# Scores of two heads side by side in TensorE's row halves, in an attention and mixture-of-experts kernel

## The chip, the cores and the metric

The kernel runs on one core of a Trainium2 chip (trn2). The time is the device time of one launch in microseconds: median of three runs 371.16 us (371.13 to 371.59). A profile is one more execution, recorded by the hardware profiler. Engines in its views: PE is TensorE's matmuls, PEld its weight loads (which overlap the matmuls), DVE is VectorE, ACT is ScalarE, POOL is GpSimd, SP is the sync engine that issues DMAs.

## The reference

Attention over 4 batches of 8 heads, 768 positions, 64 values a head; then a mixture of 4 experts, in which every token goes through every expert:

```python
scores = q @ k.T / sqrt(64)                    # batch 4, heads 8, seq 768, dim 64
keep   = causal                                # heads 0, 2, 6 ("retrieval")
keep   = causal & (first 4 keys | last 64)     # heads 1, 3, 4, 5, 7 ("streaming")
a      = softmax(where(keep, scores, -1e9))
x      = (a @ v).transpose(0, 2, 1, 3).reshape(3072, 512)
p      = domain_probs / sum(domain_probs)
out    = sum over e of p[:, e] * (relu(x @ w1[e]) @ w2[e])     # w1 512x1024, w2 1024x512
```

## The kernel before

**Work and its order.** A batch is cut into two chunks of 384 queries, so there are eight attention chunks. The expert network takes tiles of 128 tokens: the first three and the fourth one by one ("plain" steps, L1255), the other twenty in pairs (`pair_steps`, L1405). A pair has first layers (plain matmuls of 256 columns at L1413, or seven products in place of eight at L1442) and then one second layer, seven products of 16 matmuls with 256 columns each (L1596), whose intermediate sums ScalarE copies (L1616), and VectorE adds (L1619) and combines (L1175).

Each engine's instructions are written out by hand in one order; nothing is rescheduled afterwards. The main loop at the end walks through the expert network's steps, advances a planned clock (`tick`, L1154) and puts a step of the next attention chunk between them as long as a plan of due times (`plan`, L1779, and `att_ns`, L1768) says that the chunk is behind. Attention is therefore spread between the matmuls of the expert network. A generator that yields `WAIT` puts its step off. `require` (L1805) finishes a chunk at once where its result is needed.

**Scores.** `scores(h)` (L892) computes one head's scores of a chunk, with keys as the stationary operand and queries moving, into a bank of PSUM (`bank()`, L101: four banks, shared with the first layers), then lets ScalarE take the exponential into a tile `es` (L917), and VectorE multiply the mask in (L924, L928). Queries of two heads lie together in 128 rows (`qT`, 64 rows each). The keys of one head stand in a tile of 128 rows of which the other head's 64 rows are zeros (`kR` for the retrieval heads, `kW` for the windowed ones), so a matmul runs over all 128 rows and the zeros drop the other head's queries. A retrieval head has four score matmuls in the first chunk of a batch and eight in the second; a streaming head of batches 1 to 3 has seven windows of 56 (the first 48) queries.

**Where the keys come from.** In batches 1 to 3, POOL's DMAs load keys and queries of a chunk by rows and narrow them to 16 bits (`load_by_rows`, L218, three DMAs each), SP's DMAs transpose them (`transpose_rows`, L261: three for the keys into `kT`, three for the queries into `qT`), and VectorE copies the halves into their places (`keys_to_rows`, L273; `keys_to_windows`, L281). `kT` holds one chunk and the tail of the one before. `load_k` and `load_q` of the next chunk are issued when a chunk begins; the transposes of the next chunk after its fourth head.

**Values.** `values_r` (L937, retrieval heads) and `values` (L1010) multiply the weights by the values in PSUM tiles `pV`, and divide. Retrieval heads' results go through `x_one` or `x_pair` and a transposing DMA of SP's (L1004) into `xT`, the input of the expert network; the streaming heads' quotient is taken with a logarithm and an exponential on ScalarE (L1039, L1042), and VectorE's product (L1045) comes 1.3 us of planned clock later. `values` of a streaming head waits on the planned clock, so that two don't follow at once (`apart`). In batches 1 to 3 the heads go in the order 0, 2, 6, 1, 3, 5, 7, 4 (L1071), each head's values some heads behind its scores.

Batch 0 is different: its first chunk has an order of its own (`FRONT`, L619), its second transposes on TensorE (L798), with outputs in half of the array's columns.

Of the kernel before, what the change touches and what calls it, by code (L numbers as in the profile page):

```python
# [19 lines left out]
def kernel(  # L20
# [99 lines left out]
    for i in range(2):  # L120
        kR.append(pers.tile([P, NCH, NR, 3, P], FP16, name=f"kR{i}"))
        vR.append(pers.tile([P, S // P, NR, D + 2], FP16, name=f"vR{i}"))
# [38 lines left out]

    kT = pers.tile([P, HP, P + CH], FP16, name="kT")
    v_sinks = pers.tile([NS, 1, NSH * P], FP16, name="v_sinks")
# [16 lines left out]
    def key_tile(b, c, h, t):  # L180

        i = b % 2
        if RETR[h]:
            return kR[i][:, t // 3, RH.index(h), t % 3, :]
        if b:
            return kW[:, t, SH.index(h), :]
        return kS[:, t // TC, t % TC, SH.index(h), :]
# [29 lines left out]

    def load_by_rows(x, x16, b, c):  # L218
        for j in range(3):
            s0 = c * CH + j * P  # L220
            gp.dma_start(
                out=x16[:, j, :, :],
                in_=x[b, :, s0 : s0 + P, :].rearrange("h p d -> p h d"),
            )
# [36 lines left out]
    def transpose_rows(b, c):  # L261
        alloc_qT(b, c)
        for x, xr, at in ((kT, k_rows[b, c], P), (qTs[b, c], q16[b, c], 0)):
            for j in range(3):
                nc.sync.dma_start(
                    out=x[:, :, at + j * P : at + (j + 1) * P],
                    in_=xr[:, j, :, :].rearrange("p h d -> p (h d)"),
                    transpose=True,
                )
# [3 lines left out]
    def keys_to_rows(b, c):  # L273

        for n, hps in ((slice(0, 2), slice(0, 2)), (slice(2, 3), slice(3, 4))):
            nc.vector.tensor_copy(
                out=kR[b % 2][half(0), c, n, :, :].rearrange("p n t x -> p n (t x)"),
                in_=kT[half(0), hps, P : P + CH],
            )

    def keys_to_windows(b, c, part):  # L281

        x = kW[:, 0:WT, :, :]
        for r, n0, hp0, n in [((1, 0, 0, 2), (1, 3, 2, 2), (0, 2, 2, 1))[part]]:
            r = half(r)
            src = kT[r, hp0 : hp0 + n, P - WO + NS :]
            step = src.ap[1][0]
            src = bass.AP(
                src.tensor, src.offset, [src.ap[0], [step, n], [WQ, WT], [1, P - NS]]
            )  # L290
            dst = x[r, :, n0 : n0 + n, :].rearrange("p t n x -> p n t x")
            nc.vector.tensor_copy(out=dst[:, :, :, NS:P], in_=src)
            if c == 0:
                src = kT[r, hp0 : hp0 + n, P : P + NS]
                src = src.rearrange("p n (t x) -> p n t x", t=1)
                nc.vector.tensor_copy(
                    out=dst[:, :, :, 0:NS], in_=src.to_broadcast([D, n, WT, NS])
                )
        if part == 2 and b * NCH + c + 1 < G:
            nc.vector.tensor_copy(out=kT[:, :, P - WO : P], in_=kT[:, :, CH + P - WO :])  # L300

# [478 lines left out]
    def attention(b, c):  # L780
# [111 lines left out]
        def scores(h):  # L892
            hp = h // 2
            es_of[h] = []
            for cols, parts, masks in score_tiles(h):
                ps = bank()
                ns = 0
                for n, (t, o, q0, nq) in enumerate(parts):
                    nc.tensor.matmul(  # L899
                        out=ps[:, o : o + nq],  # L900
                        lhsT=key_tile(b, c, h, t),
                        rhs=qTs[b, c][:, hp, q0 : q0 + nq],
                        start=(n == 0 or not first),
                        stop=not first,
                        skip_group_check=first,
                    )
                    ns += mm_ns(nq)
                if first:
                    for m, mo, o0, o1 in masks:
                        bias = bC if m is mC else bSf  # L910
                        nc.tensor.matmul(
                            out=ps[:, o0:o1], lhsT=ident16,
                            rhs=bias[:, mo : mo + o1 - o0],
                            start=False, stop=True, skip_group_check=True,
                        )
                es = att.tile([P, 512], FP16, name="es", bufs=8)
                nc.scalar.activation(  # L917
                    out=es[:, 0:cols], in_=ps[:, 0:cols], func=AF.Exp, scale=SC
                )
                for m, mo, o0, o1 in () if first else masks:  # L920
                    if m is mC:
                        x = es[:, o0:o1].rearrange("p (n x) -> p n x", x=P)
                        y = mC.rearrange("p (n x) -> p n x", n=1)
                        nc.vector.tensor_tensor(  # L924
                            out=x, in0=x, in1=y.to_broadcast(list(x.shape)), op=ALU.mult
                        )
                        continue
                    nc.vector.tensor_tensor(  # L928
                        out=es[:, o0:o1],
                        in0=es[:, o0:o1],  # L930
                        in1=m[:, mo : mo + o1 - o0],
                        op=ALU.mult,
                    )
                es_of[h].append((es, parts))
                yield ns

        def values_r(h):  # L937

            ct, u = PLACE[h]
            shared = by_dma and ct  # L940
# [69 lines left out]
        def values(h):  # L1010
# [3 lines left out]
            ct, u = PLACE[h]  # L1014
            while by_dma and clock[0] < apart["until"] and not apart["rush"]:
                yield WAIT
# [32 lines left out]
            later(scale, g)  # L1049
            apart["until"] = clock[0] + 1900.0  # L1050

            yield ns + (600.0 if g == 1 else 400.0)
# [17 lines left out]
        else:  # L1070
            order = (0, 2, 6, 1, 3, 5, 7, 4) if by_dma else (0, 2, 1, 3, 6, 5, 7, 4)  # L1071
            more = divmod(g + 1, NCH) if g + 1 < G else None
# [6 lines left out]
            if by_dma:  # L1079
                keys_to_rows(b, c)  # L1080
                yield 1500.0
            else:
                yield from transposes(0)

            waiting = []
            for n, h in enumerate(order):
                v_steps, done = iter(()), None
                ahead = sum(len(score_tiles(x)) for x in (*waiting, h))
                if len(waiting) > 1 or (waiting and ahead > (6 if by_dma else 8)):
                    done = waiting.pop(0)  # L1090
                    v_steps = values(done)
                yield from both(scores(h), v_steps)
                if not by_dma and n < 2:
                    yield from transposes((1, 3)[n])
                if done is not None:
                    behind_values(done)
                waiting.append(h)
                if n < 3 and by_dma:
                    keys_to_windows(b, c, n)
                if n == 1 and by_dma:  # L1100
                    sink_rows(b, c)
                if n == 3 and more and g > 1:
                    transpose_rows(*more)
                if not by_dma and n == 2:
                    yield from transposes(2)
            if more:
                if g == 1:
                    load_probs(pair0)
                    transpose_rows(*more)
            for h in waiting:  # L1110
# [37 lines left out]
    WAIT = -1.0  # L1148
    apart = {"until": 0.0, "rush": False}

    def later(op, g):
# [253 lines left out]
    def pair_steps(nt0, nxt):  # L1405

        def plain_layer1(e):
            xs = scaled(e)
            for f0 in range(0, FTP, 2):
# [19 lines left out]
                yield 2 * DMP * mm_ns(PC), 0.5  # L1429

        s1 = moe.tile([P, 4 * HN], FP32, name="s1", tag="sums", bufs=1)
        kept = [s1[:, (n % 2) * HT * P : (n % 2 + 1) * HT * P] for n in range(3)]
# [210 lines left out]
        if ahead and three(nxt):  # L1643
            inputs_for_third()
        half = KT // 2 * mm_ns(HN), PSHARE
        yield from product(x, A11, b(0, 0), True)
        keep(0, x)
# [37 lines left out]
        if last:  # L1685

            r = slice((nt0 + 1) * P, (nt0 + 2) * P)
            for c in (slice(0, HN // 2), slice(HN // 2, HN)):
# [12 lines left out]
                nc.sync.dma_start(out=out[r, c], in_=o[:, 1, c])  # L1701
            return
        yield from product(x, A22, t(2), False)
        nc.scalar.copy(out=o[:, 1, 0:HN], in_=x)
# [48 lines left out]
    zero(gp, kR[1].rearrange("p c n t x -> p (c n) t x"))  # L1753
    gp.memset(kT[:, :, P - WO : P], 0.0)

# [12 lines left out]
    def att_ns(a):  # L1768
        ns = 4000.0 if a % NCH == 0 else 6100.0
        ns += 1000.0 if a >= NCH else 0.0  # L1770
        ns += NSH * (600.0 if a == 1 else 400.0)
        return ns + (600.0 + HP * 3 * 400.0 if a < NCH else 0.0)

# [4 lines left out]
    begin = E * UNIT + 0.6 * ONE  # L1778
    for a, n in zip(range(2, G), (0.72, 1.65, 2.95, 4.15, 5.4, 6.65)):  # L1779
        plan[a] = (begin, first_pair + n * PAIR)  # L1780
        begin = plan[a][1]
# [90 lines left out]
```

## Time and profile before

| | |
|---|---|
| median of three runs | 371.16 us |
| the profiled execution's own time | 370.57 us |
| its span, first to last instruction | 368.8 us |
| granted TensorE clock, mean | 1.000 |
| PE matmuls, 60 to 180 us / 180 to 368.8 us | 120.00 of 120.00 us / 185.82 of 188.80 us |
| VectorE in the same stretches | 92.55 / 140.96 us |
| ScalarE | 81.86 / 105.02 us |
| POOL | 57.77 / 17.43 us |
| score matmuls, L899 | 396 recorded, 141 on `kR` and 255 on `kS` |
| first chunk of batch 1 begins (copies at L276) | 78.4 us |

A PE record's end is modelled, so records of neighbours overlap, and a busy share near 1 says only that matmuls were always in flight. The distance between starts tells what a matmul cost. VectorE and ScalarE have room over the whole, which says nothing of a single moment.

### The profile page before, as it was taken

What the parts mean: (1) busy time and instruction counts of PE and PEld (TensorE: products, weight loads), DVE (VectorE), ACT (ScalarE), POOL (GpSimd) and SP (SyncE); (2) the same over time, 40 slices, a digit from 0 to 9 for tenths busy, and PEclk for the clock granted to TensorE, in tenths of its full rate; (3) what the DMA queues carried; (4) which work ended last, traced back from release to release, by engine and by line L of the source; (5) the groups of instructions that cost most, each with busy time, mean ns of one, the idle gap of its engine ahead of it and who ended that gap; (6) DMA issues with size and microseconds to landing.
All of it is one profiled execution on the core that took longest, in us unless ns stands there. A gap on an engine that the chain in (4) does not pass through costs nothing.

```text
span 368.8 us, 10367 instructions
## 1 busy us (share of the span) xinstructions
PE 362.9 (98%) x4243; PEld 309.6 (84%) x4243; DVE 278.0 (75%) x586; ACT 227.0 (62%) x477; POOL 120.6 (33%) x176
## 2 busy tenths in 40 slices
PE   7999999999999999999999999999999999999996
PEld 4755566679999999999989999988999998998996
DVE  7864875898687499778567749777758868979982
ACT  6736689348768776765767955874777361450630
POOL 7985775783166049027302731220000000000000
PEclk9999999999999999999999999999999999999999
DMA  8999999999999399999907992960220300300101
GB/s 222 193 199 206 185 195 195 168 183 116 138 93 164 93 108 141 122 120 106 150 11 90 168 129 40 124 126 2 71 69 2 116 3 2 117 2 0 60 3 57
DMA packets 119092, 39.55 MB, mean 107 GB/s; under 512 B 107024, under 2 KB 111700, under 8 KB 119044
## 3 DMA queue, kind: packets, MB, share of 16 engines
q0 software_dynamic: 82848, 18.62, 60.1%
q1 hardware_dynamic: 35108, 19.48, 24.4%
q10 hardware_dynamic: 1088, 0.79, 0.7%
q8 instruction: 33, 0.54, 0.6%
q14 instruction: 15, 0.12, 0.1%
HBM read 44.89 MB, written 6.34 MB: 139 GB/s over the span
## 4 chain that ended last, share of the span: by engine, by line
PE 86%; DMA 5%; DVE 4%; POOL 3%; issue 1%; DVEq 0%
PE pO L1596 30%; PE pA L1413 21%; PE pO L1442 9%; PE pO L1294 6%; PE pA L1247 6%; PE pA L899 5%; DMA w1sb<-in_moe_w_dram 2%; PE pV L1442 2%; PE pA L1442 2%; PE pV L957 2%; PE pV L1024 2%; DVE xs L1361 1%; DMA xT<-x_pair 1%; DMA hA<-in_k_dram 1%; POOL w1sb L330 1%; DMA hA<-in_q_dram 1%
## 5 line engine op out<-in xcount | busy, mean ns | idle before, releaser
L1596 PEld LDWEIGHTS <-hA 128*128 128x128 f16 x1104 | 104.6, 98 | 11.8
L1413 PE MATMUL pA<-xs,w1sb 128*128 128x256 f16 x768 | 97.3, 272 | 0.0
L1413 PEld LDWEIGHTS <-w1sb 128*128 128x128 f16 x768 | 71.8, 98 | 7.3
L1596 PE MATMUL pO<-w2sb,hA 128*128 128x256 f16 x640 | 77.3, 272 | 0.0
L1422 ACT ACTIVATE hA<-pA 128x512 f16<-128x512 f32 x96 | 57.1, 598 | 29.1 <-PE pA L1413 26.9
L917 ACT ACTIVATE es<-pA 128x384 f16<-128x384 f32 (+2 forms) x122 | 58.5, 513 | 21.3 <-PE pA L899 19.3
L308 POOL DMA_DIRECT2D vS<-in_v_dram x30 | 29.6, 989 | 107.4 <-PE pV L1024 105.6
L1596 PE MATMUL pO<-tsb,hA 128*128 128x256 f16 x464 | 57.0, 272 | 0.0
L1361 DVE TENSOR_TENSOR xs<-xT,pB 128x1024 f16<-128x1024 f16 (+1 forms) x49 | 46.9, 978 | 2.8 <-DMA xT<-x_pair 2.8
L1175 DVE TENSOR_TENSOR hA<-hA 128x1024 f16<-128x1024 f16 x60 | 39.2, 684 | 0.5 <-PE pO L1596 0.3
L1442 PEld LDWEIGHTS <-w1sb 128*128 128x128 f16 x512 | 31.3, 98 | 1.3 <-DVE xs L1175 0.4
L1274 ACT ACTIVATE hA<-pA 128x128 f16<-128x128 f32 (+1 forms) x59 | 19.4, 377 | 19.9 <-PE pA L1247 19.6
L1294 PE MATMUL pO<-w2sb,hA 128*128 128x512 f16 x120 | 28.9, 379 | 0.0
L1247 PE MATMUL pA<-xT,w1sb 128*128 128x128 f16 (+1 forms) x236 | 27.8, 268 | 0.3 <-DMA w1sb<-in_moe_w_dram 0.3
L1616 ACT COPY s<-pO 128x256 f32<-128x256 f32 x31 | 11.6, 373 | 26.2 <-PE pO L1596 20.6
L1247 PEld LDWEIGHTS <-w1sb 128*128 128x128 f16 x256 | 19.3, 98 | 9.1 <-issue 1.2
L1045 DVE TENSOR_TENSOR xT<-pV,rc 64x384 f16<-64x384 f32 x35 | 19.4, 555 | 9.9 <-ACT rc L1042 9.2
L1039 ACT ACTIVATE rc<-pV,eps 64x384 f32<-64x384 f32 x35 | 20.1, 576 | 9.7 <-PE pV L1024 9.2
L1459 DVE CUSTOM_DVE_ANT_0 hA<-pO,s 128x512 f16<-128x512 f32 x26 | 17.7, 688 | 9.8 <-PE pO L1442 8.3
L928 DVE TENSOR_TENSOR es<-es,mS 128x384 f16<-128x384 f16 (+1 forms) x40 | 13.7, 346 | 14.9 <-ACT es L917 14.9
L1452 ACT COPY s<-pO 128x512 f32<-128x512 f32 x39 | 22.7, 588 | 2.7 <-PE pO L1442 2.3
L899 PE MATMUL pA<-qT,kR 128*128 128x128 f16 (+2 forms) x141 | 23.2, 261 | 0.0
(194 smaller groups left out, 536.9 us busy)
## 6 DMA issues: line engine op xcount, KB each, us to landing
pB<-p_rows SPq DMA_DIRECT2D x10, 512.0 KB, 7.2
out_dram<-o SPq DMA_DIRECT2D x19, 256.0 KB, 3.9
w1sb<-in_moe_w_dram POOLq DMA_DIRECT2D x16, 256.0 KB, 7.3
w2sb<-in_moe_w_dram POOLq DMA_DIRECT2D x8, 512.0 KB, 8.5
vS<-in_v_dram POOLq DMA_DIRECT2D x30, 112.0 KB, 3.9
k_rows<-in_k_dram POOLq DMA_DIRECT2D x18, 128.0 KB, 5.0
q<-in_q_dram POOLq DMA_DIRECT2D x18, 128.0 KB, 6.4
out_dram<-hA SPq DMA_DIRECT2D x4, 256.0 KB, 7.1
```

The lines of the kernel that those rows point to most:

```text
L308: gp.dma_start(out=t[:, :, own_v(h)], in_=windows_of(v, b, h, c))
L899: nc.tensor.matmul(out=ps[:, o : o + nq], lhsT=key_tile(b, c, h, t), rhs=qTs[b, c][:, hp, q0 : q0 + nq], start=(n == 0 or not first), stop ...
L917: nc.scalar.activation(out=es[:, 0:cols], in_=ps[:, 0:cols], func=AF.Exp, scale=SC)
L1175: nc.vector.tensor_tensor(out=out, in0=a, in1=b, op=ALU.subtract)
L1247: nc.tensor.matmul(out=ps[:, 0 : x.shape[2]], lhsT=w1_tile(e, CTS[n], ft), rhs=x[:, CTS[n], :], start=(n == 0), stop=(n == DMP - 1),)
L1294: nc.tensor.matmul(out=ps_o, lhsT=hs[:, ft, :].rearrange("p (x j) -> p j x", j=tiles)[:, j, :], rhs=w2sb[:, e * FTP + ft, :], start=(ft == 0),
L1361: nc.vector.tensor_tensor(out=o, in0=xin, in1=pb.to_broadcast([P, DMP, n, P]), op=ALU.mult)
L1413: nc.tensor.matmul(out=ps[:, f * PC : (f + 1) * PC], lhsT=w1_tile(e, ct, f0 + f), rhs=xs[:, ct, :], start=(ct == 0), stop=(ct == DMP - 1),)
L1422: nc.scalar.activation(out=blocks[:, b0 : b0 + 2, k0 : k0 + 2, :].rearrange("p t f x -> p f t x"), in_=ps.rearrange("p (f t x) -> p f t x" ...
L1442: nc.tensor.matmul(out=ps[:, f * P : (f + 1) * P], lhsT=w_tile(e, w[:, ct, :], f), rhs=a[:, ct, :], start=(first and f == 0 and ct == 0), ...
L1452: nc.scalar.copy(out=kept[n], in_=ps)
L1596: nc.tensor.matmul(out=ps, lhsT=a[:, k, :], rhs=b(k), start=(first and k == 0), stop=(k == KT - 1), skip_group_check=not first,)
```

## The change

In batches 1 to 3:

- Heads 0 and 2 (`TURNED`), 1 and 3, and 4 and 5 (`WINDOWED`) get their queries and keys in the two row halves of the same tile: `SLOT` puts head 2 beside head 0, and head 1 in place of it. Their score matmuls use 64 rows each, in turns of the two heads, into different banks (`scores_of_two`). Four banks are written in one go, and then their four exponentials are queued.
- A go is only begun while `wide["open"]` holds, which the second layers of a pair set and the first layers clear (it is set at the start), and when the planned clock says that ScalarE is nearly free (`by_act`).
- `kT` keeps a whole batch of keys. Heads 0 and 2 read it as it is, the windowed pairs read windows copied with both heads at once and without zero rows; heads 6 and 7 (`PADDED`) keep zero rows.
- The order within a chunk is written out anew (`in_pairs_of_heads`): goes first, then values, with heads 6 and 7 in between. The transposes of the next chunk come after the scores of all heads and the values of 0, 2, 6 and 1.
- Loading by rows takes seven DMAs in place of three, since the slots of heads 0 to 3 are out of order.
- Exponentials of heads 1, 3, 4 and 5 lie in a part of `kS` that is no longer used for keys. The plan's numbers are changed.

```diff
-    kT = pers.tile([P, HP, P + CH], FP16, name="kT")
+    kT = pers.tile([P, HP, WO + S], FP16, name="kT")
+    SLOT = (0, 2, 1, 3, 4, 5, 6, 7)
+    TURNED, WINDOWED, PADDED = (0, 2), ((1, 3), (4, 5)), (6, 7)
...
     def key_tile(b, c, h, t):
...
+        if b and h in PADDED:
+            return kR[1][:, t // 3, b % 2, t % 3, :] if RETR[h] else kW[:, t, 4, :]
+        if b:
+            r, hp = half(SLOT[h] % 2), SLOT[h] // 2
+            if RETR[h]:
+                return kT[r, hp, WO + t * P : WO + (t + 1) * P]
+            return kW[r, t, [h in x for x in WINDOWED].index(True), :]
...
     def load_by_rows(x, x16, b, c):
+        for h in range(HP):
+            gp.dma_start(out=x16[:, :, SLOT[h], :], in_=rows_of(x, b, h, c))
         for j in range(3):
             s0 = c * CH + j * P
             gp.dma_start(
-                out=x16[:, j, :, :],
-                in_=x[b, :, s0 : s0 + P, :].rearrange("h p d -> p h d"),
+                out=x16[:, j, HP:, :],
+                in_=x[b, HP:, s0 : s0 + P, :].rearrange("h p d -> p h d"),
             )
...
     def keys_to_rows(b, c):
-        for n, hps in ((slice(0, 2), slice(0, 2)), (slice(2, 3), slice(3, 4))):
+        nc.vector.tensor_copy(
+            out=kR[1][half(0), c, b % 2, :, :].rearrange("p t x -> p (t x)"),
+            in_=kT[half(0), 3, WO + c * CH : WO + (c + 1) * CH],
+        )
...
+    def keys_to_windows(b, c, n):
+        r, hp = ((slice(0, P), 1), (slice(0, P), 2), (half(1), 3))[n]
+        src = kT[r, hp, c * CH + NS :]
+        src = bass.AP(src.tensor, src.offset, [src.ap[0], [WQ, WT], [1, P - NS]])
+        dst = kW[r, 0:WT, (0, 1, 4)[n], :]
+        nc.vector.tensor_copy(out=dst[:, :, NS:P], in_=src)
...
             for cols, parts, masks in score_tiles(h):
+                while by_dma and by_act["free"] > clock[0] + 900.0 and not apart["rush"]:
+                    yield WAIT
...
+        def exponentials(h, ps, cols, parts, masks):
+            if by_dma and h in (1, 3, 4, 5):
+                n = (1, 3, 4, 5).index(h)
+                n = (2 + n // 2) * NT * P + n % 2 * CH
+                es = kSf[:, n : n + CH]
+            else:
                 es = att.tile([P, 512], FP16, name="es", bufs=8)
...
+            by_act["free"] = max(by_act["free"], clock[0]) + 650.0
+            ready[h] = by_act["free"] + 500.0
...
+        def scores_of_two(work):
+            while not (wide["open"] and by_act["free"] < clock[0] + 500.0):
+                if apart["rush"]:
+                    break
+                yield WAIT
+            done, ns = [], 220.0
+            for heads, (n, parts, masks) in work:
+                pss = [bank() for _ in heads]
+                for t, o, q0, nq in parts:
+                    for h, ps in zip(heads, pss):
+                        nc.tensor.matmul(
+                            out=ps[:, o : o + nq],
+                            lhsT=key_tile(b, c, h, t),
+                            rhs=qTs[b, c][half(SLOT[h] % 2), SLOT[h] // 2, q0 : q0 + nq],
+                            start=True,
+                            stop=True,
+                        )
+                    ns += mm_ns(nq)
+                done += [(h, ps, n, parts, masks) for h, ps in zip(heads, pss)]
+            for x in done:
+                es_of.setdefault(x[0], [])
+                exponentials(*x)
+            yield ns
+
+        def in_pairs_of_heads():
+            keys_to_rows(b, c)
+            tiles = score_tiles(TURNED[0])
+            work = [[(TURNED, x) for x in tiles[n : n + 2]] for n in range(0, len(tiles), 2)]
+            others = [(x, *score_tiles(x[0])) for x in WINDOWED]
+            yield from scores_of_two(work[0])
+            keys_to_windows(b, c, 0)
+            keys_to_windows(b, c, 1)
+            yield 200.0
+            for x in (*work[1:], others):
+                yield from scores_of_two(x)
+                yield 100.0
+            keys_to_windows(b, c, 2)
+            sink_rows(b, c)
+            yield from values(0)
+            yield from both(scores(6), values(2))
+            yield from values(6)
+            yield from both(scores(7), values(1))
+            behind_values(1)
+            if more:
+                transpose_rows(*more)
+            for h in (3, 4, 5, 7):
+                yield from values(h)
+                behind_values(h)
...
+            while not soon(h):
+                yield WAIT
...
     def att_ns(a):
-        ns = 4000.0 if a % NCH == 0 else 6100.0
...
+        if a == 1:
+            return 6700.0 + NSH * 600.0 + HP * 3 * 400.0
+        return 5300.0 if a % NCH == 0 else 7300.0
...
-    for a, n in zip(range(2, G), (0.72, 1.65, 2.95, 4.15, 5.4, 6.65)):
+    for a, n in zip(range(2, G), (0.6, 1.5, 2.55, 3.95, 5.2, 6.65)):
```

`soon(h)` is true when the planned clock has passed `ready[h]`; `values` of a streaming head asks it too, and adds 1200 to `by_act["free"]`.

## The prediction

> **What bounds the kernel now.** First the page's busy line and the chain that ended last:
>
> ```profile
> PE 362.9 (98%) x4243; PEld 309.6 (84%) x4243; DVE 278.0 (75%) x586; ACT 227.0 (62%) x477; POOL 120.6 (33%) x176
> PE 86%; DMA 5%; DVE 4%; POOL 3%; issue 1%; DVEq 0%
> ```
>
> TensorE's matmuls hold 86% of the chain, and the waiting of DMA, VectorE and POOL in it lies mostly before 30 us. So from batch 1 on, a microsecond of TensorE work removed is a microsecond of time, as long as TensorE does not wait in its place. The second view is TensorE's order of time in a stretch without gaps. Columns: start, length with a modelled end, line, operation, count. The distance from one start to the next is the true price:
>
> ```profile
> 151.84 0.34 PE L899 MATMUL pA<-qT,kS 128*128 128x48 f16 x7
> 152.03 0.61 PE L1442 MATMUL pO<-xs,w1sb 128*128 128x128 f16 x8
> 152.47 1.04 PE L1413 MATMUL pA<-xs,w1sb 128*128 128x256 f16 x8
> 153.34 0.34 PE L957 MATMUL pV<-vR,es 128*128 128x65 f16 x6
> ```
>
> Seven matmuls of a windowed head (48 and 56 columns) take 152.03 - 151.84 = 0.19 us, 27 ns each; 128 columns take 0.44/8 = 55 ns, 256 take 0.87/8 = 109 ns. Price goes by columns; that half of the contraction rows are zeros in these scores makes nothing cheaper. The third view is the same list where batch 0 uses half of the array's columns (128*64, two outputs in two halves):
>
> ```profile
> 46.59 0.82 PE L1247 MATMUL pA<-xT,w1sb 128*128 128x384 f16 x4
> 47.25 0.19 PE L957 MATMUL pV<-vR,es 128*128 128x65 f16 x1
> 47.37 0.36 PE L798 MATMUL pA<-ident,q 128*64 128x128 f16 x6
> 47.56 0.33 PE L798 MATMUL pA<-ident,k 128*64 128x128 f16 x6
> 47.83 0.61 PE L1294 MATMUL pO<-w2sb,hA 128*128 128x512 f16 x2
> ```
>
> From 47.25 to 47.83 are 0.58 us, 0.03 of them for the 65 columns. Twelve matmuls of 128 columns in turn would be 12 x 55 ns = 0.66 us, more than there is. Side by side they are 6 x 55 = 0.33 us, and 0.22 us remain for going into the half-array shape and back.
>
> **The change part by part.** *TensorE work removed.* A turned head (0 or 2) has four matmuls in a first chunk (128, 128, 256, 256 columns: 0.33 us) and eight in a second (1,920 columns: 15 x 55 = 0.82 us). Heads 0 and 2 side by side save one of the two: 3 x (0.33 + 0.82) = 3.45 us over three batches. The pairs (1,3) and (4,5) save one windowed head each, 0.185 us, in six chunks: 12 x 0.185 = 2.2 us. Together 5.65 us. The trace has no row halves; the nearest row is L798's column halves. Bounds: nothing saved, and 5.65. I take 5.65, since L798 overlapped fully.
>
> *Shape changes added.* A first chunk has two goes (one for the turned heads, one for the windowed), a second chunk three: 3 x 5 = 15 goes, each into and out of the shape, at L798's 0.22: +3.3 us. Bounds: the way in alone costs 0.12 - 0.03 = 0.09 (47.25 to 47.37), so 1.4 us if the way out is free; 5.7 us if each way costs a whole small matmul's latency (0.19).
>
> *Four banks in one go.* ScalarE must empty four banks after each go. Its back-to-back pace is:
>
> ```profile
> 111.08 1.47 ACT L917 ACTIVATE es<-pA 128x512 f16<-128x512 f32 x3 [0.49 <-PE pA L899]
> ```
>
> Three in 1.47 us with 0.60 for one alone: the next two take about 0.44 to 0.48 each. So four full banks are free about 0.27 + 0.60 + 3 x 0.48 = 2.3 us after the first of them is written, and that one is written 0.2 us before the go ends. In a second layer the next go stands at least two half products (1.74 us) and a shape change (0.1) on and uses its fourth bank last: no wait. The copies of the product (L1616) queue behind the exponentials, but the bank they empty is wanted again one whole product (1.74 us) later: hidden. In the first chunk of batch 1 the built order of the changed kernel puts the goes into the plain layers, the first 0.86 us before a first layer, which also needs these banks at 0.22 us each, the second right behind that layer's eight ReLUs. Going bank by bank, the third and fourth are about 0.1 us late each and the second go's fourth bank 0.3: +0.5 us. Bounds: 0, and 1.4 if the activations don't overlap at all (0.60, 0.60, 0.39, 0.39 and 0.28 per ReLU).
>
> *Queues of SP and POOL.* The transposes of the next chunk now stand behind the x_pair transpose of heads 2 and 6, and the next chunk's first go comes at once:
>
> ```profile
> 126.00 3.84 SPq L265 DMA_TRANSPOSE kT<-k_rows  x3
> 129.93 4.32 SPq L265 DMA_TRANSPOSE qT<-q  x3
> 134.34 1.21 SPq L1004 DMA_TRANSPOSE xT<-x_pair  x1
> ```
>
> Each takes 1.3 us of the queue, and a qT one lands 3.6 us after issue (kT: 4.8). From the end of head 6's values: 1.2 us to x_pair, 1.3 for its transpose, 6.55 until the last qT issue, 3.6 to land: 12.7 us. In the changed order the matmuls between that end and the next go are worth 14.2 us (batch 1), 12.9 (batch 1 to 2), and over 18 later. The one at 12.9 has no margin: +0.3 us, bounds 0 and 1.5 (VectorE up to a microsecond late). In exchange the x_pair transpose no longer waits behind the six. Before, it did once on the chain:
>
> ```profile
> 229.45 1.20 DVE xs L1361 x2
> ...
> 235.99 4.06 DMA xT<-x_pair
> 243.98 1.75 PE pA L1413 x16
> ```
>
> It landed at 240.05, its scaling came late, and TensorE's records have a gap of 0.31 us at 241.6: -0.3 us, bounds 0 and -0.8 (all gaps after 60 us).
>
> POOL issues 48 loads of three rows and 36 of four in place of 36 of eight, at 0.79 against 0.91 us: 67 us for 33, 5.7 us more per chunk:
>
> ```profile
> L221 POOL DMA_DIRECT2D q<-in_q_dram x18 | 16.3, 928 | 0.8 <-issue 0.8
> L306 POOL DMA_DIRECT2D vR<-in_v_dram x21 | 16.1, 786 | 4.7 <-DMA w2sb<-in_moe_w_dram 3.9 <-DMA k_rows<-in_k_dram 0.7
> L308 POOL DMA_DIRECT2D vS<-in_v_dram x30 | 29.6, 989 | 107.4 <-PE pV L1024 105.6 <-DMA k_rows<-in_k_dram 1.3 <-DMA q<-in_q_dram 0.5
> ```
>
> Its 105.6 us of waiting for values matmuls (up to 20 at a time) hide that; without this cover the queries of the second chunk of batch 1, landing at 96 to 101 where they are turned from 97 on, would cost up to 1 us. VectorE loses 7.5 us of copies (6 x 0.465 to kR, 12 x (0.646 - 0.402) to the windows, 1.2 of repeated sinks, 5 x 0.245 of carried keys); it is not on the chain there: nothing.
>
> **Sum.** -5.65 + 3.3 + 0.5 + 0.3 - 0.3 = -1.85 us. The profiled execution took 370.57 us around its span of 368.8 and lies 0.59 below the median of 371.16. Its time would be 368.7, the median's 369.3.
>
> **Rivals.** *(a) The halves overlap only partly.* In the windowed pairs a matmul lasts 27 ns and each wants its own weight load. If the loads of both halves go in turn, a pair of 56 columns lasts 54 ns and the 2.2 us vanish: 371.16 - 1.85 + 2.2 = 371.5. For it: seven loads in 0.19 us is also 27 ns a load, so the present pace may be that of loading. Against: L798's pairs keep 55 ns with two loads in them. [...]
>
> *(b) The burst is not hidden: slower.* One mechanism: ScalarE's four exponentials in a row, at every go. Masks on VectorE wait for them, and the second layers' copies (0.37), additions (0.42) and differences (0.68) stand behind in both queues. If each go makes TensorE wait 0.25 us, that is 15 x 0.25 = 3.75: 373.1. It decides from 1.85/15 = 0.12 us per go. For it: four windowed exponentials and their masks (0.35) end some 2.0 us after the go, an addition 0.42 later, and in the last batches it is wanted 2.6 us after the go: a margin of 0.2. Against: before, ScalarE is 62% busy, and its copies ran freely. [...]
>
> *(c) It doesn't do what it says:* the halves don't overlap at all. Then nothing is saved and the costs stay: 371.16 + 3.3 + 0.5 + 0.3 - 0.3 = 375.0. Against it stands L798; for it, that those halves share all 128 rows and these don't.
>
> **How the numbers follow.** Forecast 369.3: 0.54. Its own range goes from 367.4 (-5.65 + 1.4 + 0.5, the way out of the shape free and the two terms of 0.3 cancelling) to 370.4 (half of what the waits' upper bounds leave: (0.9 + 1.2)/2 = 1.05 more). (a) 371.5: 0.19. (b) 373.1: 0.20. (c) 375.0: 0.07. About 0.2%, 0.74 us, is what this kernel's measurement can tell from no change. Faster is the forecast, 0.54; of (a) 0.15 lies within 0.74 us; slower is the rest of (a), (b) and (c): 0.31. The range goes from 367.4 to 373.2, which takes in (a) and most of (b) and leaves out (c) and the tails.
>
> **What would show it.** Pairs right: two matmuls of a turned go start a few ns apart, with 55 or 109 ns to the next pair, and a windowed go has 28 matmuls in about 0.38 us. Shape changes right: 0.22 us over the matmuls' own time per go. The burst: gaps before the matmul that takes a bank, copy or sum behind an exponential, none in second layers, some 0.5 us around the two goes of batch 1's first chunk. SP: the first go of batch 2 waits for qT by less than 1.5 us, and the 0.31 us gap is gone. I am wrong if windowed pairs keep 54 ns, if a change of shape by rows costs over 0.35 us a go, or if second layers show waits of over 0.12 us per go.

## The result, and the profile after

The changed kernel took 375.72 us in the median of six executions (375.05 to 378.32), the kernel before 371.33 beside it: 1.0127 times as long, interval 1.0092 to 1.0162. It is slower by 4.4 us, where 2 us of gain were forecast.

The profiled execution took 378.32 us, its span 376.6 against 368.8 before. Its busy line and the engines' shares of the chain that ended last:

```profile
PE 365.4 (97%) x4243; PEld 306.2 (81%) x4243; DVE 274.2 (73%) x575; ACT 226.3 (60%) x477; POOL 149.6 (40%) x224
PE 61%; DMA 19%; POOL 10%; issue 6%; SPq 2%; DVE 2%; ACT 1%; POOLq 0%; ACTq 0%; DVEq 0%
```

The number of matmuls is the same (x4243), yet TensorE's share of the chain fell from 86% to 61%, and DMA's rose from 5% to 19%. The 19% are not all lost time: from 42 to 81 us the chain follows loads and transposes back while TensorE works. What TensorE loses are its waits for transfers. Who it waited for is in the view of waits (engine, line, releaser, us in total, times, longest):

```profile
PE pA L963 <- DMA qT<-q: 4.9, 2, 2.9
...
PE pO L1506 <- DVE xs L1238: 1.0, 1, 1.0
```

L963 is the matmul of a go. The two waits are the first goes of batch 1 and of batch 2. The chain in order of time (start, length, what) shows the first, then the second:

```profile
71.24 1.19 SPq L273
...
74.69 6.26 DMA qT<-q
80.95 0.14 issue
81.09 0.51 PE pA L963 x8
```

```profile
137.57 4.74 DMA qT<-q
142.31 0.04 issue
142.35 0.51 PE pA L963 x8
```

TensorE had reached these goes at 77.8 and 140.1 us. From start to start of its matmuls, the two waits are 3.07 and 2.12 us over the matmuls' own time. The third query transpose took 6.3 and 4.7 us from issue to landing, not the 3.6 of the prediction. What stood ahead of it on SP's queue the second time:

```profile
128.55 1.19 SPq L1071 DMA_TRANSPOSE xT<-x_pair  x1
129.96 3.83 SPq L273 DMA_TRANSPOSE kT<-k_rows  x3
134.01 4.79 SPq L273 DMA_TRANSPOSE qT<-q  x3
```

Before, x_pair came behind the six; now the six come behind it, and the last query transpose is issued at 137.57. A third stop is at 249 us, where the kernel before had its gap of 0.31:

```profile
246.46 2.55 DMA out_dram<-o
249.02 0.11 DVE xs L1424
...
250.55 0.62 PE pO L1506 x8
```

TensorE loses 1.20 us there. The releaser named, a store of results, is inferred from its time, and VectorE's scaling does not read it. In the code, the buffer written at L1424 is `xs1`, which takes the room of the rows of queries, `q16` (L1270). It may be written when the last three query transposes have read them, and those stood on SP's queue from 240.32 on, behind x_pair:

```profile
234.83 1.25 SPq L1071 DMA_TRANSPOSE xT<-x_pair  x1
236.30 3.81 SPq L273 DMA_TRANSPOSE kT<-k_rows  x3
240.32 5.26 SPq L273 DMA_TRANSPOSE qT<-q  x3
```

In the DMAs' completion records the last of them ends at 248.58, and the scaling begins 0.42 us later, at 249.00. `e2_three_loads` below has the same 0.42 us, from 246.10 to 246.52. So the change of SP's order comes back here as well.

A fourth loss is in the table by stretches (stretch, length, busy us of PE, PEld, DVE, ACT and POOL with counts, then granted TensorE clock, DMA share, GB/s):

```profile
77.70:81.10 3.40, 0.49 (x5) 0.04 (x3) 2.03 (x3) 0.00 (x0) 3.01 (x7) 1.00 1.70 177
81.10:85.00 3.90, 3.90 (x30) 2.67 (x31) 2.35 (x6) 2.47 (x7) 3.74 (x5) 0.57 1.09 180
85.00:140.00 55.00, 54.99 (x718) 48.34 (x716) 39.51 (x84) 42.25 (x85) 30.85 (x41) 1.00 1.21 120
140.00:142.40 2.40, 0.45 (x6) 0.24 (x6) 1.97 (x4) 1.02 (x3) 2.40 (x4) 1.00 1.52 96
142.40:147.00 4.60, 4.60 (x55) 3.20 (x55) 2.78 (x8) 2.44 (x7) 4.60 (x7) 0.63 1.24 85
```

After each of the two waits for queries TensorE ran 3.41 us at half clock (a granted clock of 0.50 from 81.68 to 85.10 and from 143.12 to 146.54; matmuls of 512 columns 427 ns apart, of 128 columns 107, against 216 and 56 at a clock of 1.00). By the table the loss is 3.9 x 0.43 + 4.6 x 0.37 = 3.4 us. Not every execution shows it: mean clocks were 0.991, 0.995, 0.999 and three times 1.000, with 378.32, 377.34, 375.06 us and 375.05 to 376.0. So the median of 375.72 lies among the executions at 1.000: the kernel is slower without the half clock too. Other runs have such waits too: the one of 2.94 us in `e12_before_go_early` was followed by a clock of 0.63 from 81.5 to 86 us, while those of 2.24 (`e1_turn_early`), 2.17 (`e2_three_loads`) and 3.13 us (`e6_windows_first`) were not followed by such a stretch in the profiled executions, whose mean clocks are 1.000, 0.999 and 0.999 (3.41 us at 0.50 would lower a mean over 375 us by 0.005). So the length of the wait alone does not tell whether half clock follows: 2.12 us had it and 3.13 us had not. What decides it was not tested.

The bill of the profiled execution: waits 3.07 + 2.12 + 1.20 = 6.4 us, half clock 3.4, together 9.8; the span grew by 7.8, so the rest gained about 2.0 us net. Most of that is the halves, which `e9_full_rows` below puts at 1.5 us. TensorE's list of a second layer (start, length with a modelled end):

```profile
110.20 0.61 PE L963 MATMUL pA<-qT,kT 64*128 64x128 f16 x10
110.75 1.05 PE L1660 MATMUL pO<-tsb,hA 128*128 128x256 f16 x8
...
115.02 0.53 PE L963 MATMUL pA<-qT,kS 64*128 64x48 f16 x28
115.49 1.05 PE L1660 MATMUL pO<-w2sb,hA 128*128 128x256 f16 x8
```

From 110.20 to 110.75 are 0.55 us for ten matmuls that would take 0.88 in turn, and 28 windowed ones take 0.47 for 0.71. By the starts, the way into the shape costs 0.096 us and the way out 0.09.

### The profile page after: what moved, and what is told of

Same layout as the page of the kernel before. It is cut to its first block, busy times and chain, and to the rows that moved or that the text cites. A ratio compares the mean times of both kernels' runs of the same rounds, so it can differ in the third digit from the quotient of the medians.

```text
span 376.6 us, 10434 instructions
## 1 busy us (share of the span) xinstructions
PE 365.4 (97%) x4243; PEld 306.2 (81%) x4243; DVE 274.2 (73%) x575; ACT 226.3 (60%) x477; POOL 149.6 (40%) x224
## 4 chain that ended last, share of the span: by engine, by line
PE 61%; DMA 19%; POOL 10%; issue 6%; SPq 2%; DVE 2%; ACT 1%; POOLq 0%; ACTq 0%; DVEq 0%
PE pO L1660 27%; PE pA L1476 16%; PE pO L1506 8%; DMA q<-in_q_dram 3%; DMA k_rows<-in_k_dram 3%; DMA qT<-q 3%; DMA w1sb<-in_moe_w_dram 2%; DMA w2sb<-in_moe_w_dram 2%; PE pV L1506 2%; SPq L273 2%; PE pA L963 2%; PE pA L1506 2%; POOL w1sb L329 1%; DMA vS<-vS 1%; POOL q L226 1%
## 5 line engine op out<-in xcount | busy, mean ns | idle before, releaser
L1660 PEld LDWEIGHTS <-hA 128*128 128x128 f16 x1104 | 105.4, 98 | 14.8 <-issue 2.1
L1476 PE MATMUL pA<-xs,w1sb 128*128 128x256 f16 x768 | 95.8, 273 | 0.0
L927 ACT ACTIVATE es<-pA 128x512 f16<-128x512 f32 (+3 forms) x98 | 45.2, 520 | 21.5 <-PE pA L900 12.5
L307 POOL DMA_DIRECT2D vS<-in_v_dram x30 | 28.2, 943 | 74.2 <-PE pV L1093 70.5
L1424 DVE TENSOR_TENSOR xs<-xT,pB 128x1024 f16<-128x1024 f16 (+1 forms) x49 | 46.8, 977 | 3.2 <-DMA out_dram<-o 3.1
L1357 PE MATMUL pO<-w2sb,hA 128*128 128x512 f16 x120 | 29.8, 387 | 0.0
L1310 PE MATMUL pA<-xT,w1sb 128*128 128x128 f16 (+1 forms) x236 | 28.9, 275 | 0.0
L1451 DVE TENSOR_TENSOR hA<-hA 128x1024 f16<-128x1024 f16 (+1 forms) x26 | 14.6, 563 | 15.0 <-ACT hA L1485 14.8
L1357 PEld LDWEIGHTS <-hA 128*128 128x128 f16 x128 | 12.5, 103 | 11.9 <-issue 0.9
```

Of the source, the lines that this page charges most:

```text
L307: gp.dma_start(out=t[:, :, own_v(h)], in_=windows_of(v, b, h, c))
L927: nc.scalar.activation(out=es[:, 0:cols], in_=ps[:, 0:cols], func=AF.Exp, scale=SC)
L1310: nc.tensor.matmul(out=ps[:, 0 : x.shape[2]], lhsT=w1_tile(e, CTS[n], ft), rhs=x[:, CTS[n], :], start=(n == 0), stop=(n == DMP - 1),)
L1357: nc.tensor.matmul(out=ps_o, lhsT=hs[:, ft, :].rearrange("p (x j) -> p j x", j=tiles)[:, j, :], rhs=w2sb[:, e * FTP + ft, :], start=(ft == 0),
L1424: nc.vector.tensor_tensor(out=o, in0=xin, in1=pb.to_broadcast([P, DMP, n, P]), op=ALU.mult)
L1476: nc.tensor.matmul(out=ps[:, f * PC : (f + 1) * PC], lhsT=w1_tile(e, ct, f0 + f), rhs=xs[:, ct, :], start=(ct == 0), stop=(ct == DMP - 1),)
```

## The experiments

All ran beside the kernel before; on their chip that took 370.8 to 370.9 us. "Early", "windows first" and "later go" are the three edits that are put together below.

**One edit of SP's order (`e1_turn_early`).**

```diff
             yield from both(scores(6), values(2))
+            if more:
+                transpose_rows(*more)
             yield from values(6)
             yield from both(scores(7), values(1))
             behind_values(1)
-            if more:
-                transpose_rows(*more)
```

> The changed kernel, with one statement moved: the six transposes of the next chunk are issued before the values of head 6, so that they stand ahead of the x_pair transpose on SP again, as in the kernel before. TensorE's order is the same to the last matmul. Theory (late queries): TensorE's wait of 2.1 us before the first go of batch 2 and the 1.2 us gap at 249 us (there VectorE writes into the room of the queries' rows, which the last three transposes must have read) both come from these transposes being late, so 3.3 us go and at most 0.3 us come back for x_pair: 372.4 to 373.0 us against the 375.7 of the changed kernel; the wait of 3.1 us before the first go of batch 1 stays, since that chunk's transposes are issued elsewhere. Rival (shape changes and bursts of exponentials cost more than costed): these are untouched, so 375.4 to 376. Rival (POOL's fourteen loads alone make the queries late): the waits stay where they are, 375.4 to 376.

372.85 us, ratio 1.0067 (1.0043 to 1.0091). The wait for queries at batch 2 and the gap at 249 are both gone from the trace, with TensorE's order unchanged: the theory held, and the third stop was SP's order too. The room of `q16` alone was not tried. What the late queries had hidden now shows:

```profile
PE pA L963 <- DVE kS L297: 2.4, 3, 1.2
PE pA L963 <- DMA qT<-q: 2.1, 1, 2.1
```

L297 copies windows for the second go of a chunk. It is emitted behind the first go and stands behind masks and the experts' additions in VectorE's queue.

**Fewer loads (`e2_three_loads`).**

```diff
-        for h in range(HP):
-            gp.dma_start(out=x16[:, :, SLOT[h], :], in_=rows_of(x, b, h, c))
...
-                out=x16[:, j, HP:, :],
-                in_=x[b, HP:, s0 : s0 + P, :].rearrange("h p d -> p h d"),
+                out=x16[:, j, :, :],
+                in_=x[b, :, s0 : s0 + P, :].rearrange("h p d -> p h d"),
```

> The changed kernel with three DMAs per load of queries or keys, as before, in place of seven. Heads 1 and 2 then lie in each other's places, so the outputs are those of exchanged queries and keys; instructions, shapes and their number are otherwise the same. Theory (late queries): the queries of the first chunk of batch 1 are loaded some 5.7 us sooner, and TensorE's wait of 3.1 us before the first go of batch 1 falls under 1 us; the wait at batch 2 and the gap at 249 us stay: 372.6 to 373.8 us. Rival (SP's queue alone is late, POOL's loads are hidden as the prediction said): all three stay, 375.4 to 376.

376.29 us, ratio 1.0166 (1.0106 to 1.0227). The theory fell: TensorE still waited 2.17 us at the first go of batch 1. POOL issued the queries by 59.1 us in place of 69.5, yet by the completion records the third transpose ended at 80.07 us in place of 80.95. In the kernel before it had ended at 80.48, 8.6 us after its issue at 71.89. So these queries land at 80 to 81 us in each of the three; the kernel before did not notice, since its first scores start at 82.08:

```profile
69.03 4.14 SPq L265 DMA_TRANSPOSE qT<-q  x3
...
82.08 0.39 PE L899 MATMUL pA<-qT,kR 128*128 128x128 f16 x3
```

The rival, by which all three stops stay, does not hold either: the gap at 249 us is not in this trace, the wait for queries at batch 2 is 0.49 us, and a wait of 1.46 us for queries at 109 us is new.

**The loads alone (`e4_before_seven_loads`)**, in the kernel before:

```diff
+        for h in range(HP):
+            gp.dma_start(out=x16[:, :, h, :], in_=rows_of(x, b, h, c))
...
-                out=x16[:, j, :, :],
-                in_=x[b, :, s0 : s0 + P, :].rearrange("h p d -> p h d"),
+                out=x16[:, j, HP:, :],
+                in_=x[b, HP:, s0 : s0 + P, :].rearrange("h p d -> p h d"),
```

> The kernel before with seven DMAs per load in place of three, natural order, nothing else. Theory (late queries need both late loads and an early go): its first scores of batch 1 stand some 6 us behind the landing of their queries, so the loads' 5.7 us are hidden and the time is 371.0 to 371.8 us. Rival (POOL's loads alone cost the time): TensorE waits for qT or for values behind the loads here too, 372.5 to 374.5 us.

371.24 us, ratio 1.0012 (0.9997 to 1.0026). POOL's extra issues are hidden, as the prediction had them.

**Holding back the goes of batch 1's first chunk, two ways.** In `e3_early_and_wait` with early transposes:

```diff
+            begun = clock[0]
+            while clock[0] < begun + {2: 3300.0}.get(g, 0.0) and not apart["rush"]:
+                yield WAIT
             yield from scores_of_two(work[0])
```

> The changed kernel with the transposes issued before head 6's values, and the first go of batch 1 held back by 3.3 us of planned clock, by which it stands 3.5 us of matmuls later in TensorE's order (the second go of that chunk then falls into the next second layers, 16 us later). Theory (late queries): no go waits for queries, TensorE's clock stays at 1.000, and what is left is the saving by halves less the shape changes: 369.0 to 370.4 us, under the 371.3 of the kernel before. Rival (shape changes or bursts eat the saving): no wait for queries, but 371.5 or more. Rival (a shift of the goes only moves the wait to the second chunk of batch 1, whose transposes are now later too): a wait for qT before the go at about 105 us, 371 to 373.

387.28 us, ratio 1.0449 (1.0424 to 1.0473). The wait moved and grew, as the last rival has it, but to far more: the second go fell behind the next first layer, values and the next transposes behind it, and the queries of the next two chunks were late by 6.55 and 4.24 us.

```profile
PE pA L963 <- DMA qT<-q: 10.5, 2, 6.4
```

In `e5_later_go`, on the changed kernel as it is, the second go was also let into a first layer, so that nothing is pushed on:

```diff
-            while not (wide["open"] and by_act["free"] < clock[0] + 500.0):
+            while not ((wide["open"] or g == 2) and by_act["free"] < clock[0] + 500.0):
...
+            begun = clock[0]
+            while g == 2 and clock[0] < begun + 3300.0 and not apart["rush"]:
+                yield WAIT
             yield from scores_of_two(work[0])
```

> The changed kernel with the two goes of batch 1's first chunk held back: the first stands 3.5 us of matmuls later in TensorE's order, the second 2.6 us later, for which that chunk's goes may also fall into a first layer. Nothing else of the order changes. In the kernel before, the last query transpose of this chunk was complete at 80.3 us and its first scores began at 82.08; the changed kernel reached the go at 77.8 and the transpose was complete at 80.6. Theory (an early go meets queries that land at 80 to 81 us in every kernel): the wait of 3.1 us falls under 0.7, the wait at batch 2 and the gap at 249 us stay: 372.2 to 373.6 us. Rival (the queries are late because the changed kernel loads and turns them late, and go on being late): at most 1 us gained, 374.5 to 376.

374.52 us, ratio 1.0111 (1.0070 to 1.0152), 0.9 above the theory's range and at the lower end of the rival's; the interval overlaps that of the changed kernel, so a gain is not shown. The trace speaks for the theory all the same: the first go of batch 1 no longer waits for queries. (The 80.3 and 80.6 us in the expectation are not the last completion records of those transfers; these are at 80.48 and 80.95.) But TensorE is now earlier at the next chunk, whose queries were not late before:

```profile
102.91 5.64 DMA qT<-q
108.56 0.04 issue
108.60 0.61 PE pA L963 x10
```

1.20 us are lost there, 1.36 for window copies at batch 2 and 0.59 at 245 us. So the late queue gives back much of what one wait less had gained.

**An early first score without the change (`e12_before_go_early`)**: the kernel before, one number of the plan changed.

```diff
-    begin = E * UNIT + 0.6 * ONE
+    begin = E * UNIT + 0.2 * ONE
```

> The kernel before, with the first chunk of batch 1 begun earlier in the plan (begin at E * UNIT + 0.2 * ONE in place of 0.6): its first score matmul stands at 72.35 us of TensorE's work in place of 76.73, where the changed kernel has its first go (72.30). Loads, keys, SP's order and full rows as before. Theory (the early go is what costs the 3.1 us, whoever makes it, since this chunk's queries are complete only at 79 to 82 us): TensorE waits 2 to 4 us before the first score of batch 1, for keys or queries, and the time is 372.3 to 375 us. Rival (it takes the changed kernel's loads, layout or goes to be late): no wait of over 0.7 us there, 370.5 to 371.5 us.

375.42 us, ratio 1.0106 (1.0077 to 1.0135), 0.4 above the range. With the old loads, full rows and SP's old order, TensorE waits 2.94 us, and the chain has the same shape as in the changed kernel:

```profile
72.66 8.69 DMA qT<-q
81.34 0.14 issue
81.48 0.38 PE pA L899 x3
```

The stretch after it, from 81.5 to 86 us, ran at a clock of 0.63. This one step, made alone, costs as much as the whole change. It settles the first wait: the go is too early for queries that land at 80 to 82 us whether the loads, the rows and SP's order are old or new.

**Copies of windows first (`e6_windows_first`)**: early, and

```diff
-            yield from scores_of_two(work[0])
             keys_to_windows(b, c, 0)
             keys_to_windows(b, c, 1)
+            yield from scores_of_two(work[0])
             yield 200.0
```

> The kernel with early transposes (372.85 us), and the two copies of windows on VectorE ahead of the first go of a chunk in place of behind it. In the kernel with early transposes TensorE waited 1.36 us before the windowed go of batch 2's first chunk and 1.2 us before that of batch 1, both times for these copies, which stood behind masks and the experts' additions in VectorE's queue. Theory (late copies, a wait that the late queries had hidden): the 1.36 us go, and some of the 1.2: 370.3 to 371.6 us. Rival (VectorE's backlog is the cause, and copies put ahead only push the masks and additions back): within 0.6 us of 372.85.

371.77 us, ratio 1.0030 (1.0004 to 1.0056), 0.2 above the range. No go waits for copies any more; the wait for queries at batch 1 is left, 3.13 us. Of its ten executions six at a clock of 1.000 took 370.13 to 371.91 us, four at 0.994 to 0.999 took 373.08 to 374.46. Half clock is only part of that difference: one stretch as in the changed kernel, 3.41 us at 0.50, would cost 1.7 us and lower the mean clock to 0.995, and the profiled execution, 373.36 us at 0.999, has full clock around its wait. What else made it long is open.

**All three edits (`e7_all_three`)**: early, windows first, and the later goes of `e5_later_go`.

> Early transposes, windows ahead of the first go, and the goes of batch 1's first chunk held back. Theory: no go waits by more than 0.7 us, the halves save 5.6 us and fifteen changes of shape cost 2.8 (0.186 us each, by the starts in the trace of the changed kernel): 368.0 to 369.6 us, against 370.8 of the kernel before on this chip. Rival (bursts of exponentials and masks, or the copies, take the saving): 370.4 or more with waits of over 0.12 us in each go.

370.19 us, ratio 0.9978 (0.9962 to 0.9993): 0.2% faster than the kernel before, with an interval that just leaves out 1, though 0.6 above the theory's range and 0.2 short of the rival's. TensorE waits for no query. What is left are waits for banks and for results of VectorE: 0.60 us at 84.5, 0.21 at 89.5, 0.13 at 145.4, 0.33 at 150.4 and 0.31 at 224.4, together 1.6. The last one shows the burst, and what stands behind it in VectorE's queue:

```profile
220.76 0.33 PE pA L963 x14
221.10 1.64 ACT kS L927 x4
...
222.75 0.36 DVE kS L938
...
224.33 0.43 DVE o L1686
224.75 0.04 issue
224.80 1.03 PE pO L1663 x8
```

Four exponentials, a mask, and only at 224.33 the addition for which the next product waits. For the waits at 89.5, 145.4 and 150.4 the burst is not shown to be the cause.

**The halves taken out (`e9_full_rows`)**, on all three edits. With `True`, `key_tile` returns all 128 rows:

```diff
-                            lhsT=key_tile(b, c, h, t),
-                            rhs=qTs[b, c][half(SLOT[h] % 2), SLOT[h] // 2, q0 : q0 + nq],
+                            lhsT=key_tile(b, c, h, t, True),
+                            rhs=qTs[b, c][:, SLOT[h] // 2, q0 : q0 + nq],
```

> The kernel with all three edits (370.19 us), with the matmuls of its goes over all 128 rows: the same order, count, columns and banks, keys and queries of both heads of a tile, so each of the two heads gets the sum of both heads' scores, and the outputs are those of such scores. No halves, so no overlap and no changes of shape. Theory (what the halves are worth net): by the starts, the fifteen goes take 9.34 us with halves and would take 11.16 at full price, so 1.8 us more, 371.5 to 372.6. Rival (the order written out anew, not the halves, gives what is gained): within 0.5 us of 370.19.

371.68 us, ratio 1.0021 (1.0010 to 1.0032): 1.5 us more than with halves, as the theory has it (its 1.8 less 0.3). The same go in both traces, without halves and with:

```profile
111.23 0.88 PE L964 MATMUL pA<-qT,kS 128*128 128x48 f16 x28
111.96 1.03 PE L1664 MATMUL pO<-w2sb,hA 128*128 128x256 f16 x8
```

```profile
111.34 0.53 PE L963 MATMUL pA<-qT,kS 64*128 64x48 f16 x28
111.81 1.05 PE L1663 MATMUL pO<-w2sb,hA 128*128 128x256 f16 x8
```

0.73 us to the next product against 0.47, and 0.096 of the difference is given back on the way in. Of the waits left in the kernel with all three edits, three stay without the halves: 0.53 us at 84.4, 0.21 at 150.6 and 0.22 at 225.3, together 1.0 of 1.6. So most of them belong to the new order and not to the halves.

**One head after the other (`e8_halves_in_series`)**, on all three edits:

```diff
-                for t, o, q0, nq in parts:
-                    for h, ps in zip(heads, pss):
+                for h, ps in zip(heads, pss):
+                    for t, o, q0, nq in parts:
```

> The same, but the matmuls of a go are issued one head after the other, all of the first head's and then all of the second's, in place of in turns. The same matmuls, halves, banks and shape changes, but neighbours in the queue want the same rows, except where the heads meet. By the starts, if each matmul takes its own time the goes last 5.58 us longer in all. Theory (the halves run side by side fully when issued in turns): 4.3 to 5.6 us more than the kernel with turns. Rival (the overlap is partial, the windowed pairs held back by loading weights): 2.5 to 4 us more.

370.26 us, ratio 0.9972 (0.9953 to 0.9991): no slower than in turns, which neither theory had. A windowed go grew from 0.56 to 0.67 us, where its full price in turn would be 0.36 more; a turned one grew by less than 0.01. The section on the hardware shows the starts by which the overlap stays. The six longer windowed goes add some 0.7 us; the waits left behind the goes come to 0.8 us (0.42, 0.15 and 0.20) in place of 1.6, and why they are shorter is open. So the equal time does not mean that the order costs nothing.

**A little sooner (`e11_go_a_little_sooner`)**, on all three edits:

```diff
-            while g == 2 and clock[0] < begun + 3300.0 and not apart["rush"]:
+            while g == 2 and clock[0] < begun + 2500.0 and not apart["rush"]:
```

> The kernel with all three edits, with the first go of batch 1 held back by 2.5 us of planned clock in place of 3.3; both goes of that chunk then stand 0.87 us of matmuls earlier, clear of the first layer. Theory (the second go's wait of 0.6 us in the kernel with all three edits is for banks that the first layer and the exponentials share): that wait falls under 0.2, while the first go waits 0 to 0.6 us for queries that are complete at 80.5 to 81: 369.6 to 370.4 us. Rival (queries later than 81 us in this run): a wait for qT of over 0.7 us, 370.5 or more.

369.56 us, ratio 0.9961 (0.9946 to 0.9975), at the lower edge of the theory's range. The second go's wait is gone, but the first layer behind it waits 0.55 us for a bank that an exponential holds:

```profile
PE pA L1479 <- ACT kS L927: 0.4, 1, 0.4
```

So that part of the theory fell: the burst's price moved and stayed. The interval overlaps that of the three edits; both are 0.2 to 0.4% faster than the kernel before, and by how much they differ is open.

## Why the prediction was wrong

- **What bounds the kernel** was right: TensorE's work is the time as long as TensorE does not wait in its place. It did wait, for 6.4 us.
- **TensorE work removed, -5.65, and shape changes, +3.3: right in kind and sign.** Both halves run side by side, windowed pairs too: in the changed kernel's go at 115.02 us the two matmuls of a pair start within 4 ns, and the next pair 26 ns on. The shape costs 0.187 us a go, 2.8 in all. The fifteen goes of the kernel with all three edits take 9.34 us from neighbour to neighbour, those of the run without halves 11.75, with nearly the same wait for a bank in both (0.60 and 0.53): a net 2.4 us, where 2.35 were predicted. The whole run gains 1.5 us by the halves, since the waits elsewhere are longer with them (0.98 for 0.43 us in those over 0.1). Rivals (a) and (c) are out. The 375.0 of (c) is the nearest of all forecasts to the 375.72 measured; that is chance, since its halves do not overlap and these do.
- **Four banks in one go, +0.5:** too small. Once all queries are in time, 1.6 us of short waits are left, of which two, 0.60 and 0.31 us, are traced to exponentials and banks; the second lies in a second layer, where the prediction had none. Rival (b) names the mechanism, but even all 1.6 us are less than half its price of 3.75.
- **The step that failed is "Queues of SP and POOL", the +0.3 for late queries, with bounds 0 and 1.5.** It failed three times. First, it looked at the goes where the transposes had been moved, "from the end of head 6's values", and gave batch 1's second chunk 14.2 us. The first go of batch 1 has its transposes from another place of the code, and nobody had moved them; the go had moved, 4.4 us of matmuls ahead of the first scores before (72.30 for 76.73). In the kernel before these queries landed at 80.5 us and the scores began at 82.08, 1.6 us of room. Price 3.07 us, and `e12_before_go_early` shows it without the rest. Second, "a qT one lands 3.6 us after issue" is the middle of the few landings that the profile's view of the tile `qT` gives (2.8 to 4.4 us). By the completion records of the kernel before, the eighteen took 2.4 to 9.0 us and this one 8.6; in the two waits it was 6.3 and 4.7. The chain of 12.7 us for batch 2 became 15.0, from the end of head 6's values at 127.3 to 142.3, against 12.9 at hand: 2.12 us, over the upper bound of 1.5.
- **"-0.3, x_pair no longer waits behind the six" is the third failure: wrong sign.** The transposes behind x_pair hold the room of the queries' rows, which the next inputs want: 1.20 us at 249 in place of 0.31. The 0.31 was put down to the named releaser, x_pair's landing, without asking which room the waiting instruction writes: before, the last query transpose ended at 239.88 and x_pair's at 240.09, so taking x_pair away could give 0.2 at most.
- **POOL's loads at nothing** was right (`e4_before_seven_loads`), and dropping them bought nothing (`e2_three_loads`).
- **The clock was not costed at all.** In the profiled execution of the changed kernel a stretch of half clock behind each of the waits of 3.07 and 2.12 us cost 1.7 us more. It made single executions longer, not the median.
- The slower outcome came neither from the burst nor from missing overlap, the two ways in which it had been thought of, but from a term that was given 0.3.

## What to carry to other kernels

When work is moved forward, list for each moved piece when its inputs landed in the trace of before, in that very place, and how long they then lay unused; that slack is the price list, and a median over the whole queue hid it here (3.6 us from issue to landing, against 8.6 for the one that mattered). When transfers are put behind others, ask not only who reads their result but whose room they free. The saving of small pieces on the busiest engine was real here, 1.5 us by `e9_full_rows`, but one wait of 3.07 us eats all of it, with or without half clock behind it.

## What the hardware showed that was not expected

- In `e8_halves_in_series` matmuls of one row half started before earlier ones of the other half in the queue. A windowed head's seven matmuls are queued there ahead of its neighbour's seven. Starts in ns from the go's first matmul, with columns; the first matmul of each head has 48:

```
0 48, 39 56, 64 56, 90 56, 98 48, 115 56, 136 56, 141 56, 161 56, 167 56, 187 56, 195 48, 213 56, ...
```

The second head starts at 98 ns, after four of the first head's seven, and from there two matmuls start in each 25 ns. By these records the matmuls of this go did not start in the order of the queue, across row halves.
- A change of shape cost 0.096 us in and 0.09 out by rows (L963 of the changed kernel), and much the same by columns (0.090 to 0.095 in and 0.096 out at L798 of the kernel before).
- The same DMA transpose of queries landed 2.4 to 9.0 us after its issue in the kernel before and 2.4 to 6.3 in the changed kernel, by the completion records; the one on the chain of `e12_before_go_early` took 8.7. The longest are those of batch 1's first chunk, beside POOL's loads of values; what makes them long was not tested.
- Half clock, 0.50 for 3.41 us, after each of the waits of 3.07 and 2.12 us in the profiled execution of the changed kernel, whose mean clock is 0.991; three of the other five executions of the same kernel have a mean of 1.000.
